# Attention, soft mixture of experts and a Mish layer on one core: the products of probabilities and values of a head pair written in two groups of five

## The chip, the cores and the metric

The kernel runs on one core of a Trainium2 chip. The metric is the device time of one execution in microseconds (us), as the median over several runs.

## The reference

Three layers follow one another. The attention has 4 batches, 8 heads, 576 positions and a head size of 64; the other two work on the 2304 rows of 512 that come out of it.

```python
q_rot, k_rot = (rotate(q), rotate(k))                     # rotary positions
scores = scale * np.matmul(q_rot, k_rot.transpose(0, 1, 3, 2))
attn = np.exp(scores - np.max(scores, axis=-1, keepdims=True))
attn = attn / (np.sum(attn, axis=-1, keepdims=True) + 1e-09)
x = np.matmul(attn, v)                                    # then (2304, 512)
# soft mixture of experts: softmax over rows and over slots of x @ phi,
# 8 experts of relu(slot_input @ w1) @ w2, mixed back
h = x @ w_in
out = (h * np.tanh(softplus(h))) @ w_out
```

## The kernel before

The attention works on 16 pairs of heads, one after the other; the loop index is `p`. For each pair there are nine score tiles. Tiles 0 to 7 are four blocks of 128 query positions for each of the two heads, and tile 8 holds the 64 remaining positions of both. Each tile goes through a fixed chain. TensorE (PE) multiplies queries and keys into PSUM (`s_mm`, lines 333 and 335; `s_mm2`, line 353, for tile 8). VectorE (DVE) takes the row maximum (line 361). ScalarE (ACT) takes the exponential with the sum (line 367). PE transposes the probabilities in blocks (lines 374, 388, 394, 396), and DVE or ACT copies the transposed blocks from PSUM into a tile `PT` (lines 398 to 401, 410, 413). There are two `PT` tiles for a pair: group 0 for the first 256 query positions, group 1 for the other 320.

The step that is in question here is `av(p, g, c)`: the product of the transposed probabilities with the values, for pair `p`, query group `g` and key block `c` of five. It issues two matmuls, one for each head (`h`). They write the lower and the upper 64 partitions of the same PSUM tile `m_av`, so each uses 64 of the array's 128 columns. The trace shows each such f32 matmul as two records (640 records for 320 matmuls). After the fifth block the tile is copied to `xts` (`evac`, line 410 or 413), the loads of the values for pair `p + 3` are issued (`load_v`), and `xback` (called X) transposes the result and multiplies it with `phi` (lines 449 to 457). The pool of `m_av` has one buffer, and so has `xts`. The score tiles have two PSUM buffers; the transposes, the rotated queries and keys, and X share three.

What is issued when is written in `PLAN`, one string for each of the nine steps of a pair. In it S, M and E are scores, maximum and exponential of the step's tile; T, K and R are transposes of the probabilities; V0 to V4 are `av` for group 0, W0 to W4 for group 1; X0 and X1 are `xback`; r, k and q bring the rotated inputs of the next pair through PE; a and d are their ACT and DVE halves; C is a step of a conversion of the weights `w_in` and `w_out` that runs beside the first eleven pairs or so; F is a step of the mixture's work for a batch that is done; L starts loads. A minus sign means that the action belongs to the pair before.

The written order is not the order in which an engine gets its instructions. The kernel is built with a planner (`schedule_with_timeline_sim=True`) that walks through a simulated time, and gives each engine the instruction that stands earliest in the program among those that it holds to be ready. `tc.keep_in_program_order(i)` adds one constraint: `i` comes behind the instruction that was traced just before it on its engine. It does not say that nothing may come between the two. In the attention the kernel uses it for little on PE; the last stage is pinned nearly throughout.

After the attention come the experts (lines 834 and 900), whose weights stream in by DMA, and the last layer (lines 1004 and 1038).

Of the kernel before, what the change touches and what calls it, by code (L numbers as in the profile page):

```python
# [24 lines left out]


PLAN = (
    "L T7- S M K1- E V3- V4-",
    "X0- R- C S M E",
    "S M E W0-",  # L30
    "F T0 r C S M E",
    "S a W1- W2- k F F W3- M T2 T1 E C",
    "S d q C M E",
    "S M C a E T3 W4-",
    "S a C T4 M E",
    "V0 K0 T5 d C F S F M T6 V1 E X1- d V2",
)

EVAC = {"T3": "d", "T4": "d", "K1": "a", "T0": "a", "T5": "a", "T2": "a"}
# [3 lines left out]
def kernel(  # L43
# [13 lines left out]
    nc = tc.nc  # L57
    NB, H, S, D = q.shape
    E, DM, F1 = w1.shape
# [148 lines left out]
    def load_v(p):  # L208
        b, h = divmod(2 * p, H)
        t = vs[p % 3]  # L210
        dma(
            out=t.rearrange("p h c d -> p h (c d)"),
            in_=v[b, h:h + 2, 0:512, :].rearrange("h (p c) d -> p h (c d)", c=4),
        )
        vt[p] = t
# [189 lines left out]
    def evac(dst, src, n, key=None):  # L405

        on = EVAC.get(key) or ("a" if load["a"] <= load["d"] else "d")
        if on == "a":
            load["a"] += n / 1.2 + 50
            nc.scalar.copy(dst, src)  # L410
        else:
            load["d"] += n / 0.96 + 65
            nc.vector.tensor_copy(dst, src)
# [3 lines left out]
    def av(p, g, c):  # L417
        b, hp = divmod(p, H // 2)
        n = 256 + g * R
        if c == 0:  # L420
            av_ps[p, g] = ps_a.tile([128, n], F32, tag="av", name="m_av")
        ps, pt = av_ps[p, g], PT[p, g]
        for h in range(2):
            o = 64 * h
            if c < 4:
                lhsT, rhs = vt[p][:, h, c, :], pt[:, 5 * h + c, :]
            else:
                lhsT, rhs = vrem[b % 2][:, hp, h, :], pt[:, 4, :]
            nc.tensor.matmul(ps[o:o + 64, :], lhsT=lhsT, rhs=rhs, start=(c == 0), stop=(c == 4))  # L429
        if c == 4:  # L430
            PT.pop((p, g))
            ps = av_ps.pop((p, g))
            xs = a4.tile([128, n], F32, tag="xts", name="xts")
            evac(xs, ps, n, f"X{g}")
            xts[p, g] = xs
            if g and p + 3 < NP:
                load_v(p + 3)
# [267 lines left out]
    def loads(p):  # L705
# [12 lines left out]
        "S": scores, "M": maxima, "E": expo,  # L718
        "T": lambda p, k: t_head(p, *tiles[k]), "K": t_keys, "R": lambda p, k: t_rem(p),
        "V": lambda p, k: av(p, 0, k), "W": lambda p, k: av(p, 1, k), "X": back,  # L720
        "r": lambda p, k: f_rem(p + 1), "k": lambda p, k: f_main(p + 1, "k"), "q": lambda p, k: f_main(p + 1, "q"),
        "a": lambda p, k: one(act_q), "d": lambda p, k: one(dve_q),
# [53 lines left out]
    ps = ps_m.tile([128, KDM, NSLOT], F32, tag="m", name="m_sit")  # L776
# [50 lines left out]
    for eg in range(2):  # L827
        for hf in range(2):
            end = eg == 1 and hf == 1
            for fh, cc in [(fh, cc) for fh in range(2) for cc in range(2)]:  # L830
                c = 2 * hf + cc
                for g in range(4):
# [3 lines left out]
                        rhs=parts[1, e, hf][0][:, cc * F1 + fh * 512:cc * F1 + fh * 512 + 512],  # L836
                        start=(eg == 0 and c == 0), stop=(eg == 1 and c == KDM - 1),
# [56 lines left out]
    for eg in range(2):  # L894
        for hf in range(2):
            for cc in range(4):
                c = 4 * hf + cc
                for g in range(4):
# [3 lines left out]
                        rhs=parts[2, e, hf][0][:, cc * DM:(cc + 1) * DM],  # L902
                        start=(eg == 0 and c == 0), stop=(eg == 1 and c == F1 // 128 - 1),
# [8 lines left out]
    ps = ps_m.tile([128, KDM, NSLOT], F32, tag="m", name="m_sot")  # L912
# [241 lines left out]
```

## Time and profile before

| | us |
|---|---|
| median of 3 runs | 672.29 |
| lowest and highest | 671.97, 673.31 |
| the profiled execution | 671.88 |
| its span in the trace | 670.1 |
| attention, until about | 389 |
| experts, until about | 436 |
| last layer, until the end | 670 |

In a row of the timeline stand the start, the time, the engine, the line, the operation with what it writes and reads, and how many such records are merged. "x2" at line 429 is the matmul of one head, "x4" both heads of a key block, "x12" three key blocks. The time in such a row reaches to the modelled end of the last record; how long PE was taken up is read from the start of one row to the start of the next. In square brackets stand the engine's idle time before the row and what ended it. A row of stretches gives, after the bounds and the length, the busy time (and count) of PE, PEld (weight load), DVE, ACT and POOL, then the granted clock of TensorE as a share, the DMA engines' mean busy share and GB/s.

### The profile page before, as it was taken

The numbers are of one execution on the slowest core, as the hardware profiler recorded it, in microseconds if no ns is written. First come the engines' busy times: TensorE is split into PE (matmuls) and PEld (weight loads), VectorE is DVE, ScalarE is ACT, GpSimd is POOL, SyncE is SP. The second block draws the span as 40 slices with busy tenths as digits, with TensorE's granted clock in tenths as the row PEclk, the third lists the DMA queues.
The fourth block names the chain that finished last, engine by engine and source line by source line (L and its number), as shares of the span: only waits on it lengthen the run. The fifth ranks groups of instructions, "written<-read, shape, count | busy, mean of one in ns | idle before, by whom it ended". The sixth has DMA issues, their size and how long they took to land.

```text
span 670.1 us, 11089 instructions
## 1 busy us (share of the span) xinstructions
PE 625.2 (93%) x4022; PEld 461.3 (69%) x4022; DVE 406.5 (61%) x824; ACT 336.4 (50%) x757; POOL 218.2 (33%) x263
## 2 busy tenths in 40 slices
PE   1598999989899999999999998999999999999997
PEld 1475677666577767777667653377787888888885
DVE  5777888786686866565756533177876533353342
ACT  2566776684776556665656411167765312222121
POOL 5758869755858644345400010000000000000000
PEclk9999999999999999999999999999999999999999
DMA  9678689868786965346359499962400200030004
GB/s 259 160 187 236 187 268 273 231 212 237 161 266 218 264 184 166 103 128 189 81 176 302 158 338 324 389 262 95 156 33 31 64 1 0 1 95 0 1 1 94
DMA packets 59607, 109.43 MB, mean 163 GB/s; under 512 B 12832, under 2 KB 25248, under 8 KB 59040
## 3 DMA queue, kind: packets, MB, share of 16 engines
q1 hardware_dynamic: 59552, 108.72, 54.2%
q8 instruction: 32, 0.52, 0.3%
q14 instruction: 23, 0.19, 0.1%
HBM read 70.25 MB, written 9.96 MB: 120 GB/s over the span
## 4 chain that ended last, share of the span: by engine, by line
PE 77%; DMA 9%; DVE 7%; ACT 2%; POOL 2%; issue 2%; SPq 1%; DVEq 0%; ACTq 0%; POOLq 0%
PE o_ps L1038 29%; PE m_av L429 13%; PE t L374 7%; PE s L333 5%; PE s L335 4%; PE hp L1004 3%; PE s L353 2%; DMA w<-in_moe_w_in_dram 2%; PE so_ps L900 2%; DMA w<-in_moe_w_dram 2%; DVE nmax L361 1%; PE m_lg L455 1%; PE tk L388 1%; PE m_k L285 1%; DMA w<-in_moe_w_out_dram 1%
## 5 line engine op out<-in xcount | busy, mean ns | idle before, releaser
L361 DVE TENSOR_REDUCE nmax<-s 128x1 f32<-128x576 f32 x144 | 108.0, 753 | 64.3 <-PE s L335 39.5
L367 ACT ACTIVATE P<-s,nmax 128x576 f32<-128x576 f32 x144 | 107.2, 745 | 36.3 <-DVE nmax L361 25.5
L1038 PE MATMUL o_ps<-wo_l,gh 128*128 128x512 f32 x288 | 112.9, 392 | 0.0
L1038 PE MATMUL o_ps<-wo_h,gh 128*128 128x512 f32 x288 | 112.9, 392 | 0.0
L1038 PE MATMUL o_ps<-wo_h,gl 128*128 128x512 f32 x288 | 100.7, 390 | 0.9 <-DVE gl L1019 0.9
L1011 ACT ACTIVATE room<-hp 128x512 f32<-128x512 f32 x72 | 43.0, 599 | 106.7 <-PE hp L1004 102.2
L333 PE MATMUL s<-qk_st 128*128 128x288 f32 x256 | 85.6, 349 | 10.3 <-ACT P L367 5.2
L374 PE MATMUL t<-cs,P 128*128 128x128 f32 x512 | 79.0, 282 | 4.8 <-ACT P L367 2.7
L410 ACT COPY PT<-t 128x512 f32<-128x512 f32 x92 | 53.5, 586 | 49.8 <-PE t L374 49.2
L429 PE MATMUL m_av<-PT,w 128*64 128x320 f32 (+1 forms) x384 | 73.3, 421 | 1.9 <-ACT PT L399 1.3
L374 PEld LDWEIGHTS t<-cs,P 128*128 128x128 f32 x512 | 59.6, 143 | 21.8 <-issue 9.7
L335 PE MATMUL s<-k_st,qk_st 128*128 128x288 f32 x256 | 73.8, 302 | 0.0
L333 PEld LDWEIGHTS s<-qk_st 128*128 128x128 f32 x256 | 49.9, 195 | 29.5 <-ACT P L367 9.1
L1013 DVE CAST gh<-room 128x512 fp32r<-128x512 f32 x49 | 20.9, 427 | 79.4 <-ACT room L1011 79.3
L1038 PEld LDWEIGHTS o_ps<-wo_h,gl 128*128 128x128 f32 x288 | 53.9, 188 | 13.2 <-DVE gl L1019 1.7
L231 POOL TENSOR_TENSOR w<-w,cs 128x512 f32<-128x512 f32 x34 | 45.2, 1332 | 54.1 <-PE m_k L285 46.6
L1038 PEld LDWEIGHTS o_ps<-wo_h,gh 128*128 128x128 f32 x288 | 54.1, 188 | 9.4
L1038 PEld LDWEIGHTS o_ps<-wo_l,gh 128*128 128x128 f32 x288 | 54.3, 189 | 9.0 <-DVE wo_l L891 0.2
L1019 DVE TENSOR_TENSOR gl<-room,gh 128x512 fp32r<-128x512 f32 x72 | 49.6, 691 | 4.6
L335 PEld LDWEIGHTS s<-k_st,qk_st 128*128 128x128 f32 x256 | 50.2, 196 | 0.0
L228 POOL TENSOR_TENSOR w<-w,cs 128x512 f32<-128x512 f32 x34 | 45.7, 1345 | 8.6 <-DMA w<-in_q_dram 2.9
L429 PEld LDWEIGHTS m_av<-PT,w 128*64 128x64 f32 x384 | 26.5, 136 | 23.0 <-issue 9.2
(175 smaller groups left out, 1011.5 us busy)
## 6 DMA issues: line engine op xcount, KB each, us to landing
w<-in_moe_w_dram SPq DMA_DIRECT2D x28, 1024.0 KB, 7.1
w<-in_moe_w_in_dram SPq DMA_DIRECT2D x16, 512.0 KB, 7.3
qk_st<-parth SPq DMA_DIRECT2D x46, 144.0 KB, 3.2
qk_st<-partl SPq DMA_DIRECT2D x46, 144.0 KB, 3.2
room<-in_moe_w_out_dram SPq DMA_DIRECT2D x12, 512.0 KB, 3.6
w<-in_q_dram SPq DMA_DIRECT2D x16, 256.0 KB, 5.2
w<-in_k_dram SPq DMA_DIRECT2D x16, 256.0 KB, 4.6
w<-in_moe_w_dram SPq DMA_DIRECT2D x16, 256.0 KB, 5.6
```

Source lines behind the costliest of these rows:

```text
L228: eng.tensor_tensor(out=tb, in0=src, in1=sin.to_broadcast([128, n, w]), op=ALU.mult)
L231: eng.tensor_tensor(out=dst, in0=sv, in1=cv, op=ALU.mult)
L333: nc.tensor.matmul(s[:, half, 0:288], lhsT=st[:, qc:qc + 128], rhs=st[:, KC + o:KC + o + 288], start=first, stop=False)
L335: nc.tensor.matmul(s[:, half, 0:288], lhsT=st[:, qc:qc + 128], rhs=k2_st[p % 2][:, o:o + 288], start=False, stop=last)
L361: nc.vector.tensor_reduce(out=stat[p][0][:, i:i + 1], in_=s[:, :, 0:288], axis=AX.XY, op=ALU.max, negate=True)
L367: nc.scalar.activation(out=P[p, t][:, h * S:(h + 1) * S].rearrange("p (a b) -> p a b", a=2), in_=s[:, :, 0:288], func=AF.Exp, bias=stat[p] ...
L374: nc.tensor.transpose(ps[:, j, :], P[p, t][:, blk * 128:(blk + 1) * 128], ident)
L410: nc.scalar.copy(dst, src)
L429: nc.tensor.matmul(ps[o:o + 64, :], lhsT=lhsT, rhs=rhs, start=(c == 0), stop=(c == 4))
L1011: pin(nc.scalar.activation(out=gg, in_=hp, func=AF.Mish))
L1019: pin(nc.vector.tensor_tensor(out=gl, in0=gg, in1=gh.bitcast(F32), op=ALU.subtract))
L1038: pin(nc.tensor.matmul(ops[i, n], lhsT=g_[:, cols], rhs=w_[f], start=(j == 0 and (x, k) == (0, 0)), stop=(j == NG - 1 and all(y[0] != n fo ...
```

## The change

The ten `av` steps of a pair stood in eight places of `PLAN`: V0, V1, V2 in the last step of their own pair, V3 and V4 in the first step of the next, W0 in its third step, W1 and W2, and W3, in the fifth, W4 in the seventh. They now stand in two: V0 to V4 at the end of the first step of the next pair, W0 to W4 in the fifth, ahead of k. And each matmul of `av` except the first of a group is kept behind the one before it.

```diff
 PLAN = (
-    "L T7- S M K1- E V3- V4-",
+    "L T7- S M K1- E V0- V1- V2- V3- V4-",
     "X0- R- C S M E",
-    "S M E W0-",
+    "S M E",
     "F T0 r C S M E",
-    "S a W1- W2- k F F W3- M T2 T1 E C",
+    "S a W0- W1- W2- W3- W4- k F F M T2 T1 E C",
     "S d q C M E",
-    "S M C a E T3 W4-",
+    "S M C a E T3",
     "S a C T4 M E",
-    "V0 K0 T5 d C F S F M T6 V1 E X1- d V2",
+    "K0 T5 d C F S F M T6 E X1- d",
 )
...
-            nc.tensor.matmul(ps[o:o + 64, :], lhsT=lhsT, rhs=rhs, start=(c == 0), stop=(c == 4))
+            mm = nc.tensor.matmul(ps[o:o + 64, :], lhsT=lhsT, rhs=rhs, start=(c == 0), stop=(c == 4))
+            if c or h:
+
+                tc.keep_in_program_order(mm)
```

## Rows read from the trace of the kernel before

**Rows 1.** The page's first part: busy time of each engine.
```profile
PE 625.2 (93%) x4022; PEld 461.3 (69%) x4022; DVE 406.5 (61%) x824; ACT 336.4 (50%) x757; POOL 218.2 (33%) x263
```
**Rows 2.** Stretches of the attention: early, middle, late.
```profile
84.00:106.00 22.00, 22.00 (x159) 15.95 (x159) 18.51 (x36) 16.31 (x39) 16.79 (x20) 1.00 0.91 259
...
172.00:194.00 22.00, 20.05 (x145) 14.61 (x144) 15.46 (x33) 14.69 (x36) 15.17 (x19) 1.00 0.87 240
...
282.00:304.00 22.00, 22.00 (x147) 15.29 (x146) 12.74 (x28) 13.43 (x33) 9.81 (x15) 1.00 0.47 121
```
**Rows 3.** Waits of PE, 128 to 200 us: total, times, longest.
```profile
PE t L374 <- DVE partl L273: 1.9, 1, 1.9
...
PE m_av L429 <- ACT PT L399: 1.3, 1, 1.3
```
**Rows 4.** PE's timeline: one pair's group 1 (320 columns), and what follows each piece.
```profile
277.12 0.75 PE L429 MATMUL m_av<-PT,w 128*64 128x320 f32 x2
277.81 0.40 PE L333 MATMUL s<-qk_st 128*128 128x288 f32 x1
...
279.47 1.84 PE L429 MATMUL m_av<-PT,w 128*64 128x320 f32 x12
281.24 0.66 PE L285 MATMUL m_k<-cs,w 128*128 128x128 f32 x4
281.82 0.75 PE L429 MATMUL m_av<-PT,w 128*64 128x320 f32 x2
282.51 0.66 PE L374 MATMUL t<-cs,P 128*128 128x128 f32 x4
```
**Rows 5.** PE's timeline: a tile 8, the next pair's group 0 (256 columns).
```profile
268.63 0.40 PE L353 MATMUL s<-qk_st 128*128 128x288 f32 x1
...
286.31 0.65 PE L429 MATMUL m_av<-PT,w 128*64 128x256 f32 x2
286.88 0.66 PE L374 MATMUL t<-cs,P 128*128 128x128 f32 x4
...
288.94 1.52 PE L429 MATMUL m_av<-PT,w 128*64 128x256 f32 x12
290.39 0.40 PE L353 MATMUL s<-qk_st 128*128 128x288 f32 x1
...
292.83 0.65 PE L429 MATMUL m_av<-PT,w 128*64 128x256 f32 x4
293.42 0.40 PE L333 MATMUL s<-qk_st 128*128 128x288 f32 x1
```
**Rows 6.** The last group 1, in the chain, and a copy from the timeline.
```profile
384.57 3.33 PE m_av L429 x20
...
384.55 0.37 ACT L399 COPY PT<-t 128x256 f32<-128x256 f32 x1 [1.74 <-DVE PT L398]
```
**Rows 7.** PE's timeline: four transposes ahead of scores, and ahead of a piece.
```profile
256.54 0.60 PE L374 MATMUL t<-cs,P 128*128 128x128 f32 x4
256.90 0.38 PE L333 MATMUL s<-qk_st 128*128 128x288 f32 x1
...
276.59 0.60 PE L374 MATMUL t<-cs,P 128*128 128x128 f32 x4
```
**Rows 8.** Timeline: an exponential, and scores that take its PSUM buffer.
```profile
277.90 0.75 ACT L367 ACTIVATE P<-s,nmax 128x576 f32<-128x576 f32 x1
...
282.92 0.38 PE L333 MATMUL s<-qk_st 128*128 128x288 f32 x1
```
**Rows 9.** Stretches around PE's longest wait of 128 to 200 us.
```profile
144.00:148.00 4.00, 2.13 (x18) 1.79 (x17) 3.61 (x6) 3.52 (x10) 3.33 (x4) 0.97 0.26 89
148.00:152.00 4.00, 4.00 (x22) 3.98 (x22) 2.35 (x3) 2.22 (x5) 4.00 (x4) 0.60 0.93 228
```
**Rows 10.** Stretches at the end of the attention.
```profile
376.00:386.00 10.00, 9.26 (x70) 6.87 (x71) 5.11 (x16) 3.96 (x10) 1.00 (x4) 1.00 0.26 95
386.00:396.00 10.00, 8.69 (x71) 5.92 (x68) 4.51 (x20) 2.08 (x8) 0.26 (x1) 1.00 1.03 385
```

## The prediction

> **What bounds the kernel now.** I read the engine totals first, then stretches of the attention, then the waits of PE, then PE's own timeline.
>
> The totals put PE at 93% of the span [rows 1], but an average says nothing of one stage, so I went on to stretches of 22 us, about one head pair. Late in the attention PE is busy for 22.00 of 22 us, while DVE has 12.74, ACT 13.43 and POOL 9.81 [rows 2]. PE is the bound there, with room everywhere else. From 84 to 106 us PE is full too, but DVE has 18.51 and the DMA engines 0.91 of their time. From 172 to 194 us PE has 20.05 of 22, with 15 us on POOL and 0.87 on DMA. So there are full stretches (84 to 128 and 190 to 380 us, together 234 us) and stretches in which others set the pace. The waits say the same: the long ones of PE after 128 us stand before 182 us, such as 1.9 us for a DVE subtraction and 1.3 us for a copy of probabilities [rows 3]; after that there is nothing over 0.5 us until the last pair.
>
> Since PE is always given something, a busy PE need not be an effective one. That is seen in its timeline. The reader should look at the starts in [rows 4]: a piece with one head's product ("x2") holds PE from 277.12 to 277.81, 0.69 us. Three key blocks of both heads ("x12", six times the work) hold it for 1.77 us. In group 0 one head takes 0.57 us, both heads of one block 0.59, and three blocks 1.45 [rows 5]. So the second head of a block is free if it follows the first, and a lone head costs as much as a pair of heads. From 0.69 for one block and 1.77 for three, a further block costs 0.54 us and each piece has a fixed 0.15 us. For group 0, 0.58 and 1.45 give 0.435 and 0.14.
>
> **What the change can take away.** I went through all pieces of line 429. Group 0 of every pair comes in four pieces or more (one head, one head, three blocks, one block; [rows 5] show three of them), 3.18 us in sum. The 15 groups 1 before the last come in three to five pieces, 58 in all; [rows 4] show three of the five pieces of the worst, 4.5 us, and the best are 3.14. Their mean is 3.77 us.
>
> One whole group would take 0.15 + 5 x 0.54 = 2.85 us (group 1) and 0.14 + 5 x 0.435 = 2.32 us (group 0). There is one whole group in the trace: the last of the attention holds the chain for 3.33 us, but its second head had to wait for a copy that started at 384.55 and took 0.37 us [rows 6]. Less those 0.4 us it is 2.9, as the sum says. So a pair can lose 3.77 - 2.85 = 0.92 us in group 1 and 3.18 - 2.32 = 0.86 us in group 0.
>
> Beside that each piece delays its neighbours. Four transposes hold PE for 0.36 us before scores (256.54 to 256.90), and for 0.53 before a piece (276.59 to 277.12, the first row of [rows 4]) [rows 7]: 0.17 us more. Behind scores the loss looks smaller. I take 0.1 us for each piece that goes, with ends 0 and 0.17. Group 1 loses 2.9 pieces (58 / 15 - 1), group 0 three: 0.29 and 0.30 us. If both groups became whole a pair would save 0.92 + 0.86 + 0.59 = 2.4 us (1.8 to 2.8).
>
> **What it will take away.** The plan's strings are only priorities. The pin orders the ten matmuls among themselves; it does not keep other work out. Each group must therefore be looked at by what can come between.
>
> *Group 1.* Its breaks have two causes. W0 stood in the third step, where its two heads become ready at different times: the transposed remainder is copied by DVE for one head and by ACT for the other. And W4 stood two steps behind W3, so it filled gaps as one head or one block, and earlier work took over after each. In the fifth step all ten inputs have long been copied, all ten rank ahead of k, T2, T1 and the next scores, and nothing of higher rank is left but that step's own scores. I expect one piece, at worst a lone head and the rest. Saving: 0.92 + 0.29 = 1.2 us.
>
> *Group 0.* Here the rank falls: all of it now stands behind K0, T5, the scores of tile 8, T6, X1, T7 and the next pair's first scores. It will still be used to fill gaps before those, and whatever of them becomes ready will still come between. Also, its second matmul reads what T3 leaves, and with the pins nothing of the group passes it. I expect it to stay in pieces and to lose about one of its three breaks: (0.86 + 0.30) / 3 = 0.4 us. Ends: 0 and 1.16.
>
> Sum: 1.6 us of PE time for a pair. Nothing is added: no instruction, no DMA. The value load of pair p + 3 waits for W3 as before, and PE reaches that at about the same point. X1 finds its input earlier. The `PT` tile of group 1 comes free earlier, that of group 0 is still read before T0 of the next pair, three steps on.
>
> How much of it reaches the end? In the full stretches PE waits for nobody, and the exponentials are ahead: the one at 277.90 frees its buffer by 278.7, and the scores that take this buffer start at 282.92 [rows 8], a slack of 4 us. So PE work that goes there is time that goes: 234 us / 21.8 us for a pair (tile 8 at 268.63 and 290.39 [rows 5]) = 10.7 pairs x 1.6 = 17.1 us. In the other stretches (40 to 84, 128 to 190 us) POOL, DMA or the conversion are late next; I count nothing there (ends: 0 and 1.6 for each of some five pairs, 8 us).
>
> The stages behind the attention move with it. Their weights need room that the attention gives back: DMA is 0.26 busy in the ten microseconds before its end and 1.03 right after [rows 10]. The transfers start when the attention ends, and the idle time before takes up what the last three pairs come earlier.
>
> Against the profiled execution's 671.88 us: 671.9 - 17.1 = 654.8. The median of the runs lies 0.4 us above that execution, less than I can resolve; I say 655. The forecast's own range is 646 to 664: group 0 between nothing and two breaks, and some gain in the other stretches.
>
> **Rivals.**
>
> *Both groups whole, and everywhere PE-bound.* 2.4 us x 15 pairs = 36 us: 636 (up to 42 us: 630). For it: inputs are ready early. Against it: group 0 is a filler by rank, and the stretches where DMA is at 0.9. Chance 0.11.
>
> *The change doesn't do what it says.* The planner breaks group 1 in its new place as it broke group 0 in its old one, or PE waits for as long as it saved. 672 (669 to 675). For it: the pin doesn't forbid insertion. Chance 0.12.
>
> *The fillers are missed: slower.* Today W4 and the first block of V stand as lone heads between transposes and scores, from 281.82 to 288.57, four pieces, 2 x 0.69 + 2 x 0.57 = 2.5 us. They bridge the time in which the three PSUM buffers of transposes and inputs wait for DVE and ACT. With W whole ahead of that stretch, and V held at its second matmul until T3 is copied, PE may wait there, and run V afterwards, when DVE and ACT starve. If it waits the whole 2.5 us and saves 1.6, a pair is 0.9 us longer: 15 x 0.9 = 13, so 685 (676 to 692). It decides from the point where the waits pass 1.6 us a pair. For it: DVE at 18.51 of 22 in the early stretch. Against it: the slack of [rows 8], and ACT and DVE near 13 of 22 later. Chance 0.17.
>
> *The clock falls.* Between 144 and 148 us PE was busy for 2.13 of 4 us, and from 148 to 152 us its granted clock was 0.60 on average [rows 9], between the full 2.4 GHz and the half. Such a stretch costs about 4 x 0.4 = 1.6 us. One a pair would cost 15 x 1.6 = 24 us: 655 + 24 = 679. Against it: it needs waits that the late stretches don't have. Chance 0.04. The Trainium skill has this as a rule (TensorE: Matmul & The Clock Gate, "Why this matters for your kernels"): gaps in which PE idles between bursts of matmuls send the clock to half. It speaks against two lumps with waits between them; by that rule, the trace agrees where its one long gap stands.
>
> **How the numbers follow.** Forecast 0.56, whole 0.11, nothing 0.12, fillers missed 0.17, clock 0.04. A difference under 0.2% (1.3 us) can't be told from none here. Faster: 0.56 + 0.11 = 0.67. Same: 0.12. Slower: 0.17 + 0.04 = 0.21. The range: from 638, which leaves out half of the first rival (0.05), to 682, which leaves out most of the fillers' (0.11); 0.16 in all.
>
> **What would show it.** Right: line 429 in the late attention shows rows of "x18" or "x20" with 320 columns, near 2.85 us, and the busy sum of a pair's PE falls while PE stays full; the pitch from one tile 8 to the next goes from 21.8 to about 20.1 us late in the attention. Group 0 wrong: it too is "x20". Fillers missed: PE waits for ACT or DVE copies, or for exponentials, of a microsecond and more in every pair between 200 and 380 us. Nothing: the same counts of "x2". The forecast is wrong in its base if the pieces heal and the pitch of the pairs stays.

## The result, and the profile after

| | before | after |
|---|---|---|
| median of the runs, us | 672.8 | 682.42 (678.15 to 684.94) |
| ratio | 1 | 1.013 (95% interval 1.0099 to 1.0161) |
| profiled execution, us | 671.88 | 681.91 |
| mean granted clock in it | 0.997 | 0.980 |

Slower by 1.3%, where 655 us were forecast. Everything happens in the attention: the first matmul behind it, `m_lt`, starts at 389.58 us before and at 399.79 after, and the stages that follow are as long as they were.

The totals hide it. First part of the page of after (engine, busy us, share, instructions), beside [rows 1]:

```profile
PE 626.1 (92%) x4022; PEld 470.8 (69%) x4022; DVE 408.1 (60%) x824; ACT 336.9 (50%) x757; POOL 217.8 (32%) x263
```

PE is as busy as before, although the pieces of line 429 did get fewer. PE's timeline of after, one pair's group 1 (320 columns) and the next group 0 (256), beside [rows 4, 5]:

```profile
267.95 0.75 PE L429 MATMUL m_av<-PT,v 128*64 128x320 f32 x2
268.63 0.33 PE L262 MATMUL m_rem<-cs,w 128*128 128x128 f32 x1
268.89 2.37 PE L429 MATMUL m_av<-PT,v 128*64 128x320 f32 x14
271.19 0.66 PE L285 MATMUL m_k<-cs,w 128*128 128x128 f32 x4
...
272.30 0.76 PE L429 MATMUL m_av<-PT,w 128*64 128x320 f32 x4
272.99 1.09 PE L374 MATMUL t<-cs,P 128*128 128x128 f32 x8
...
275.96 0.65 PE L429 MATMUL m_av<-PT,w 128*64 128x256 f32 x2
276.54 0.66 PE L374 MATMUL t<-cs,P 128*128 128x128 f32 x4
...
278.84 1.94 PE L429 MATMUL m_av<-PT,w 128*64 128x256 f32 x14
280.71 0.66 PE L374 MATMUL t<-cs,P 128*128 128x128 f32 x4
...
281.63 0.65 PE L429 MATMUL m_av<-PT,w 128*64 128x256 f32 x4
282.21 0.66 PE L458 MATMUL m_lg<-phi_sb,xts 128*128 128x64 f32 x4
```

The reader should look at the counts: a lone head (x2), seven matmuls (x14), the last block (x4), in both groups and in nearly every pair. Start to next start gives 0.68 + 2.30 + 0.69 = 3.67 us for group 1 and 0.58 + 1.87 + 0.58 = 3.03 for group 0. Work of lower rank stands in both gaps.

New are the waits. PE's waits of after from 50 to 401 us (total us, times, longest), beside [rows 3]:

```profile
PE s L353 <- ACT P L367: 4.2, 3, 3.4
PE s L333 <- DMA qk_st<-parth: 3.9, 2, 3.1
PE t L374 <- DVE partl L273: 3.7, 3, 3.4
...
PE m_q L285 <- POOL w L236: 1.5, 1, 1.5
```

The longest stand at 186.77 (3.42), 327.21 (3.09) and 153.48 us (3.37). Behind each the clock is down for some 6 us. Stretches of 4 us in after (busy time and instructions of PE, PEld, DVE, ACT, POOL, then the granted clock, the DMA share, GB/s):

```profile
324.00:328.00 4.00, 0.91 (x5) 0.82 (x4) 0.56 (x3) 0.37 (x1) 1.00 (x4) 0.70 0.65 147
328.00:332.00 4.00, 4.00 (x21) 3.97 (x20) 2.21 (x5) 2.02 (x5) 0.00 (x0) 0.50 0.00 0
332.00:336.00 4.00, 4.00 (x28) 2.83 (x28) 3.24 (x9) 2.43 (x7) 0.32 (x1) 0.95 0.02 4
```

A "full" PE at 0.50 does half of it: behind the wait at 186.77 us the matmuls of tile 8 follow each other at 0.24 us, behind the same tile's shorter wait in the kernel before at 0.13. PE's busy time times what is missing to a clock of 1, summed over all such stretches from 20 to 400 us, is 1.7 us before and 10.5 us after. In the totals this hides what the fewer pieces saved.

To see where time is lost I cut the attention at k's projection, which stands at the same place of each pair: the first mark (the second pair's k), the tenth mark of fifteen, and `m_lt`. "Early" is first to tenth mark, "late" from there to `m_lt`. The three of after, then those of before:

```profile
24.27 1.06 PE L285 MATMUL m_k<-cs,w 128*128 128x128 f32 x4
...
249.69 0.60 PE L285 MATMUL m_k<-cs,w 128*128 128x128 f32 x4
...
399.79 0.40 PE L583 MATMUL m_lt<-cs,c_all 128*32 128x128 f32 x2
```

```profile
24.44 1.06 PE L285 MATMUL m_k<-cs,w 128*128 128x128 f32 x4
...
239.26 0.60 PE L285 MATMUL m_k<-cs,w 128*128 128x128 f32 x4
...
389.58 0.39 PE L580 MATMUL m_lt<-cs,c_all 128*32 128x128 f32 x2
```

So all 10.6 us are lost early (214.8 to 225.4), and late nothing is won (150.3 to 150.1).

### The profile page after: what moved, and what is told of

The parts are those of the page before. It is cut to its first block, busy times and chain, and to the rows that moved or that the text cites. A ratio compares the mean times of both kernels' runs of the same rounds, so it can differ in the third digit from the quotient of the medians.

```text
span 680.1 us, 11095 instructions
## 1 busy us (share of the span) xinstructions
PE 626.1 (92%) x4022; PEld 470.8 (69%) x4022; DVE 408.1 (60%) x824; ACT 336.9 (50%) x757; POOL 217.8 (32%) x263
## 4 chain that ended last, share of the span: by engine, by line
PE 76%; DVE 8%; DMA 8%; ACT 3%; issue 2%; POOL 1%; SPq 1%; DVEq 0%; ACTq 0%; POOLq 0%
PE o_ps L1041 28%; PE m_av L429 11%; PE t L374 7%; PE s L333 5%; PE s L335 4%; DMA w<-in_moe_w_in_dram 3%; PE hp L1007 3%; DMA qk_st<-parth 3%; PE s L353 2%; PE h_ps L837 2%; PE so_ps L903 2%; PE m_lg L458 2%; DMA qk_st<-partl 1%; DVE nmax L361 1%; DVE PT L413 1%
## 5 line engine op out<-in xcount | busy, mean ns | idle before, releaser
L374 PE MATMUL t<-cs,P 128*128 128x128 f32 x512 | 81.3, 289 | 6.6 <-DVE partl L273 3.7
L374 PEld LDWEIGHTS t<-cs,P 128*128 128x128 f32 x512 | 61.8, 147 | 22.4 <-issue 11.7
L429 PE MATMUL m_av<-PT,w 128*64 128x320 f32 (+1 forms) x384 | 68.6, 425 | 0.0
L429 PEld LDWEIGHTS m_av<-PT,w 128*64 128x64 f32 x384 | 28.4, 139 | 22.0 <-issue 7.7
```

Source lines behind the costliest of these rows:

```text
L374: nc.tensor.transpose(ps[:, j, :], P[p, t][:, blk * 128:(blk + 1) * 128], ident)
L429: mm = nc.tensor.matmul(ps[o:o + 64, :], lhsT=lhsT, rhs=rhs, start=(c == 0), stop=(c == 4))
```

## The experiments

The ratios are medians of runs against the kernel before on the same chip; "early" and "late" are read off one profiled execution each.

| run | ratio (95%) | early | late |
|---|---|---|---|
| kernel before | 1 | 214.8 | 150.3 |
| the change, first comparison | 1.013 (1.010 to 1.016) | 225.4 | 150.1 |
| e5, the change again | 1.0101 (1.0068 to 1.0133) | 225.6 | 148.3 |
| e17, the change again | 1.0112 (1.0095 to 1.0129) | 225.9 | 149.5 |
| e1, weight load behind | 1.0028 (1.0007 to 1.0049) | 228.5 | 144.3 |
| e2, group 1 only | 1.0134 (1.0084 to 1.0184) | 227.4 | 150.7 |
| e3, group 0 only | 0.9958 (0.9935 to 0.9981) | 216.6 | 148.3 |
| e4, both glued | 1.0043 (1.0011 to 1.0076) | 222.1 | 149.5 |
| e6, group 0 whole | 0.9969 (0.9941 to 0.9996) | 220.8 | 145.3 |
| e7, group 1 a step later | 1.0043 (1.0009 to 1.0077) | 222.2 | 149.4 |
| e8, one wait filled | 1.0121 (1.0076 to 1.0166) | 226.1 | 148.1 |
| e9, early pairs only | 1.0119 (1.0063 to 1.0175) | 228.5 | 150.5 |
| e10, late pairs only | 0.9911 (0.9880 to 0.9942) | 217.6 | 144.4 |
| e11, late, group 0 whole | 0.9921 (0.9891 to 0.9951) | 215.0 | 144.2 |
| e12, late, both, 0 whole | 0.9973 (0.9944 to 1.0001) | 217.6 | 146.9 |
| e13, other order, no change | 1.0065 (1.0032 to 1.0098) | 218.0 | 151.2 |
| e14, other order 2, no change | 1.0010 (0.9981 to 1.0039) | 210.7 | 153.2 |
| e15, change, other order | 0.9891 (0.9848 to 0.9934) | 217.9 | 145.2 |
| e16, order of e14, late change | 0.9922 (0.9895 to 0.9949) | 209.7 | 148.4 |

The changed kernel's own split repeats within 0.5 us early and 1.8 late. Profiles of different kernels whose queues have the same order early lie up to 3.1 us apart there: before and e10 (214.8 and 217.6, every queue in the same order until 234 us), after and e1 (225.4 and 228.5). So an early part must differ by more than that to say anything. The profiled execution can lie off its kernel's median (e1's 5.4 us above, e14's 4.2 and e16's 3.4 below), so the ratio decides.

**Which half of the change, and is it a few waits or all pairs?** Theory A: a few long waits with a slow clock behind each. Theory B: every pair loses, since pieces no longer fill gaps.

e1: the load that a stage behind the attention needs is issued behind the stacked writes again.

```diff
         if p == NP - 4:
             assert not steps
+            fetch(ahead.pop(1), behind=True)
         if p == NP - 3:
...
-            for i in (0, 0, 2):
+            for i in (0, 2):
                 fetch(ahead.pop(i))
```

> The changed kernel, with one weight load (1 MB, into the room that the values' remainder of the third batch leaves) issued behind the twelve writes of stacked queries and keys of that pair instead of ahead of them. Theory A (a few long waits of PE, each with a clock fall behind it): the wait of 3.1 us before the scores at 327 us and the half clock until 332 us go, 3.1 + about 2.4 us, so 677 against 682 of the changed kernel; mean granted clock 0.985 instead of 0.98. Theory B (the loss is spread over all pairs because the pieces no longer fill gaps): the wait moves elsewhere, 681 to 683.

e2 and e3: the new priorities of one group only, no pin.

```diff
...
-    "S a W1- W2- k F F W3- M T2 T1 E C",
+    "S a W0- W1- W2- W3- W4- k F F M T2 T1 E C",
...
```

> Only group 1 (W0 to W4) moved to the fifth step; group 0 in its places of before; no pins. Theory A: it keeps the early weight load near 313 us, so a wait of 3 us and a clock fall there (5.5 us), keeps group 0's pieces ahead of tile 8's scores, so the wait of 3.4 us near 186 us shrinks to the 1.5 us of before, and saves about 0.1 to 0.2 us of pieces a pair: 674 to 677. Theory B: waits shared by the two groups alike, so half of the loss, 677 to 678, with no single wait over 2 us.

```diff
...
-    "L T7- S M K1- E V3- V4-",
+    "L T7- S M K1- E V0- V1- V2- V3- V4-",
...
```

> Only group 0 (V0 to V4) moved to the first step of the next pair; group 1 in its places of before; no pins. Theory A: no early weight load and no wait near 320 us; the wait before tile 8's scores of the seventh pair (3.4 us in the changed kernel) with its clock fall stays, 4 to 5 us, less 0.15 us of pieces a pair: 674 to 676. Theory B: half of the loss, 677 to 678, spread over the pairs.

e4: each group is to come in one piece, as the title of the change says; its nine later matmuls get the highest priority, and all ten are pinned.

```diff
+            if c or h:
+                with tc.high_priority():
+                    mm = nc.tensor.matmul(...)
...
+            tc.keep_in_program_order(mm)
```

> The changed kernel, with the first matmul of a group pinned too and the other nine at a higher priority of the planner: group 0 then runs in one piece in all pairs, group 1 in one or two. Theory A: PE work falls by a further 0.7 us (group 0) and 0.7 us (group 1) a pair, 15 to 20 us in all, of which the long waits take some back: 660 to 670. Theory B: with all pieces whole the gaps between score tiles are filled by nothing, PE waits grow in every pair: 682 to 695.

Group 1 alone costs as much as the whole change; group 0 alone gains 0.4%. Theory A had the load right (675.5 us for e1, forecast 677), but neither theory had the other three: e2 took 684.2 us (A 674 to 677, B 677 to 678), e3 671.2 (A 674 to 676, B 677 to 678), e4 677.4 (A 660 to 670, B 682 to 695). The pin does nothing: with the new priorities the compiled order of all five queues is the same with it and without. The load is worth 0.7 to 1.0% (1.0101 to 1.013 against 1.0028). SP's timeline of after shows how:

```profile
313.53 0.37 SPq L138 DMA_DIRECT2D w<-in_moe_w_dram  x1
313.99 0.47 SPq L317 DMA_DIRECT2D qk_st<-parth  x1
...
317.09 1.61 SPq L317 DMA_DIRECT2D k_st<-parth  x1
```

and of before:

```profile
304.29 0.47 SPq L317 DMA_DIRECT2D qk_st<-parth  x1
...
311.26 0.59 SPq L317 DMA_DIRECT2D qk_st<-partl  x1
311.95 0.55 SPq L138 DMA_DIRECT2D w<-in_moe_w_dram  x1
```

The 1 MB load takes the room of a value tile whose last reader is group 1's last block. Moved ahead of k, that block ends ahead of the twelve stacked writes, so the load overtakes them. The chain of waits of after holds what it costs:

```profile
313.99 7.14 DMA qk_st<-parth
...
321.21 5.41 DMA qk_st<-parth
...
327.21 0.58 PE s L333
```

The DMA view (tile, engine, count, KB, us from issue to landing) has the stacked writes at 5.2 to 7.5 us in after and at 2.5 to 3.3 before; one of them, after and then before:

```profile
k_st<-parth SPq DMA_DIRECT2D x1, 160.0 KB, 7.5
```

```profile
k_st<-parth SPq DMA_DIRECT2D x1, 160.0 KB, 3.1
```

In e1, with the load behind them, this wait is gone and the late pairs take 144.3 us. e4 leaves 1.0043. Group 0 is whole there (2.31 us where PE neither waits nor runs at a lower clock), group 1 is x16, x4 in ten of fifteen pairs and whole in five, and PE's waits over 0.3 us from 20 to 400 us sum to 35.8 us, against 18.4 before and 26.8 after.

**Group 0 whole, group 1 elsewhere, one wait filled.** e5 is the change again. e6 leaves group 1 in its old places, moves group 0, and gives its nine later matmuls the highest priority.

> The changed kernel once more, beside the others of this batch, as their measure: 1.010 to 1.016 of the kernel before, as in the first comparison (both theories). Its long waits of PE should stand at the same places: 3.4 us ahead of tile 8 of the seventh pair, 3.1 us for the stacked q and k near 327 us. If the place of a long wait changes from profile to profile, theory A (a few long waits, each with the clock at half behind it, make the loss) can't name its waits one by one.

```diff
...
+            if g == 0 and (c or h):
+                with tc.high_priority():
+                    mm = nc.tensor.matmul(...)
+                tc.keep_in_program_order(mm)
...
```

> Group 1 in the places of the kernel before; group 0 moved as in the change, and held together: its other nine matmuls get the highest priority behind the first, so it is one piece of ten in every pair, where the move alone leaves three. Ten in one piece should take PE 2.3 to 2.5 us instead of 3.03, 0.5 to 0.7 us less in each of 15 pairs. Theory A (the move of group 1 costs, through a few long waits): no new wait over 1.5 us comes up, since group 1 keeps its places, and the kernel gains those 8 to 10 us on top of the 0.4% of the move alone: 0.980 to 0.986 of the kernel before. Theory B (pieces fill gaps, and a lump leaves them open): the sum of PE's waits rises from 19 us by about as much as the pieces save, as it did when both groups were glued, and the time is 0.994 to 1.003.

```diff
...
-    "S d q C M E",
+    "S d q C M E W0- W1- W2- W3- W4-",
...
```

> Group 1 alone moved, grouped one step later than in the change (in the sixth step, behind the k projection of the next pair); group 0 as before. The 1 MB weight load that waits for the last matmul of group 1 then stands behind the twelve stacked writes of q and k again, as in the kernel before. Theory A: no wait for stacked q or k near 327 us, and the time is 0.998 to 1.006, well under the 1.013 of group 1 moved to the fifth step. Theory B (grouping itself costs, wherever it stands): 1.010 to 1.016 as in the fifth step.

```diff
+        if (p, t, blks[0]) == (6, 2, 0):
+            for _ in range(32):
+                with tc.high_priority():
+                    mm = nc.tensor.transpose(ps[:, 3, :], P[p, t][:, blk * 128:(blk + 1) * 128], ident)
+                tc.keep_in_program_order(mm)
```

> The changed kernel with 32 more transposes into a PSUM tile that has its result already (the same values again), in the seventh pair alone, just ahead of its tile 8: some 2.9 us of work for PE in the place where it waited 3.4 us for an exponential. Tile 8 is released by ACT's chain, not by PE, so it should start 12.0 us behind m_rem, as in both kernels. Theory A (the clock falls because PE stands still): the granted clock stays at 0.95 or more in the 8 us behind this wait, where it was 0.70, 0.50 and 0.94 in three stretches of 4 us, and the next pair's pitch is 2 to 3 us shorter. Rival: the clock falls for another reason (load, DMA, time): 0.5 again in the same place, although PE is busy. The time of the whole kernel moves by 2 us at most, 1.008 to 1.014.

e5 has its long waits where they were (3.37 us at 156, 3.39 at 189, 2.34 at 327 us). e6 came out as B has it, with new waits of 3.20, 2.66 and 2.24 us at 41, 66 and 108 us; e7 as A has it, without the wait near 327 us. Read by the marks they say the same: late e6 gains 5 us, early it loses 6 and e7 loses 7. So neither theory has the right cut: the loss is early, the gain late.

e8 tells what the clock is worth. The same stretches of e5, then of e8:

```profile
188.00:192.00 4.00, 2.82 (x14) 2.54 (x14) 1.80 (x4) 2.21 (x6) 3.97 (x4) 0.74 1.08 246
192.00:196.00 4.00, 4.00 (x26) 2.24 (x25) 0.93 (x5) 1.91 (x4) 1.33 (x2) 0.83 0.98 337
```

```profile
188.00:192.00 4.00, 4.00 (x35) 3.35 (x35) 1.68 (x3) 3.26 (x9) 3.63 (x4) 1.00 0.99 225
192.00:196.00 4.00, 2.75 (x23) 2.08 (x19) 2.39 (x6) 1.32 (x3) 1.51 (x2) 1.00 1.00 310
```

With PE kept busy in the wait the granted clock stays at 1.00 (2.4 GHz), so here its fall comes from PE standing still. The Trainium skill (TensorE: Matmul & The Clock Gate, "Why this matters for your kernels") says so of gaps between bursts, and this pair agrees. But the time that I expected back in the next pair did not come: tile 8 to tile 8 takes 25.03 us, against 24.88 in e5. PE now waits elsewhere:

```profile
194.20 0.37 PE L333 MATMUL s<-qk_st 128*128 128x288 f32 x1 [1.25 <-DMA qk_st<-partl]
```

The pair after that is shorter (18.36 us against 20.14), but by the tenth mark nothing is left of it: e8's early part is 226.1 us, the changed kernel's 225.4 to 225.9. The filler had a price of its own: tile 8 starts 12.7 us behind `m_rem`, where 12.0 were expected. So the 10.5 us of lost clock must not be added to the waits: here others set the pace. That a fall costs nothing is not shown by this one pair. ACT's timeline of after shows who, in the wait that e8 fills:

```profile
184.77 0.68 ACT L503 ACTIVATE w<-w 128x512 f32<-128x512 f32 x1 [2.83 <-DMA w<-in_moe_w_out_dram]
...
185.91 0.72 ACT L367 ACTIVATE P<-s,nmax 128x576 f32<-128x576 f32 x1
```

The conversion of a block of `w_out`, a weight of the last layer, waits for its load, and the exponential that tile 8 needs is queued behind it.

**Early against late.** Theory C: late, PE is the bound and fewer pieces are time; early, the change harms the queues that set the pace. Rival: the late gain is only catching up. All four kernels choose the priorities by the pair's number; in all of them the weight load stands behind the stacked writes.

```diff
         for i, step in enumerate(PLAN):
+            if p < 9 or p == 9 and not i:    # e9;  e10 to e12: p > 9 or p == 9 and i
+                step = NEW[i]
```

> The whole change in the first nine pairs alone, the places of the kernel before from the tenth pair on (the 1 MB weight load stands behind the stacked writes again). Theory C: in the early pairs POOL, DVE, ACT and the DMA queue set the pace, and the change reorders their queues, so the 8 to 11 us that k's first matmul of the eleventh pair came late (270 to 271 us instead of 260) stay, and nothing is won later: 681 to 685, 1.011 to 1.016 of the kernel before. Rival: the late pairs ran faster only because the early ones ran late (work that had been put off was done), so they catch up by themselves: 1.002 to 1.007.

> The whole change from the tenth pair on alone, with the 1 MB weight load issued behind the stacked writes as in the kernel before; the first nine pairs in the places of before, so that POOL's and SP's queues keep their order throughout. Theory C: in the late pairs PE is the bound and fewer pieces are time: the marks of k's first matmul went 85.6 us in four late pairs with the same change and the load behind, where the kernel before took 88.8, and the last pairs took 2 us less: minus 4 to minus 6 us, 0.991 to 0.994. Rival (the late gain was only catching up): 0.998 to 1.002.

> From the tenth pair on, group 0 alone in its new place and whole (ten in one piece); group 1 and the first nine pairs as before. Theory C: four late pairs took 83.4 us instead of 88.8 with group 0 whole in all pairs, and the end came 2.3 us closer behind them, so minus 6 to minus 8 us: 0.988 to 0.991. Rival (catching up): 0.997 to 1.001.

> As the run of the whole change in the late pairs, with group 0 whole besides, the load behind the stacked writes. Theory C, PE alone sets the late pairs: both savings add, 0.7 to 0.8 us a pair on top of the run without the whole group 0: minus 7 to minus 10 us, 0.985 to 0.990, the best of all. Rival: with both moved nothing is left to fill PE while it waits for DVE and ACT, and the second saving comes back as waits: 0.990 to 0.994, no better than group 0 whole alone.

C, clearly: the change in the early pairs alone costs 1.2%, in the late pairs alone it gains 0.9%. With the 0.7 to 1.0% of the load that makes 1.0 to 1.3%, which is what the whole change costs. e11 is as good as e10, a little short of C's 0.988 to 0.991: group 0 takes 2.31 us there, and group 1, left in its old places, comes out as x4, x12, x4, 3.15 us. e12 lies beyond both forecasts, on the rival's side (0.990 to 0.994): group 0 takes 2.31 us as well, but group 1 is x2, x14, x4 again, 3.67, and PE's late waits are 6.1 us against 2.3 in e10. They don't explain it: e11 has 7.3 us of them and is as fast as e10. What e12 loses is not settled. Marks of e10, beside those of after:

```profile
24.52 1.06 PE L298 MATMUL m_k<-cs,w 128*128 128x128 f32 x4
...
242.15 0.60 PE L298 MATMUL m_k<-cs,w 128*128 128x128 f32 x4
...
386.57 0.39 PE L593 MATMUL m_lt<-cs,c_all 128*32 128x128 f32 x2
```

**Why early?** The order of the queues gave the lead. In e3 ACT, POOL and SP are ordered as before and DVE differs in four places; the early part, 216.6 us, is within the spread. With group 1 moved (e2), another instruction than before stands at 379 of DVE's 824 places in the trace, at 384 of ACT's 757, 132 of POOL's 263 and 157 of SP's 386: the plan is made anew, and every engine gets another order. POOL in the second pair, after:

```profile
55.93 1.29 POOL L515 TENSOR_TENSOR w<-w,w 128x512 f32<-128x512 f32 x1 [1.15 <-ACT w L504]
57.18 1.28 POOL L228 TENSOR_TENSOR w<-w,cs 128x512 f32<-128x512 f32 x1
58.42 1.27 POOL L231 TENSOR_TENSOR w<-w,cs 128x512 f32<-128x512 f32 x1
59.65 1.29 POOL L516 TENSOR_TENSOR w<-w 128x512 f32<-128x512 f32 x1
...
61.56 0.72 POOL L236 TENSOR_TENSOR w<-w 128x256 f32<-128x256 f32 x1
```

and before:

```profile
54.55 1.28 POOL L228 TENSOR_TENSOR w<-w,cs 128x512 f32<-128x512 f32 x1
56.92 1.30 POOL L231 TENSOR_TENSOR w<-w,cs 128x512 f32<-128x512 f32 x1 [1.09 <-PE m_k L285]
...
58.86 0.90 POOL L236 TENSOR_TENSOR w<-w 128x256 f32<-128x256 f32 x1
```

Two steps of a weight's conversion (L515, L516) now stand around q's rotation, which ends at 62.28 instead of 59.76 us. q's projection waits 1.49 us for it:

```profile
62.34 0.78 PE L285 MATMUL m_q<-cs,w 128*128 128x128 f32 x4 [1.49 <-POOL w L236]
```

The stacked writes come later, and from this mark, the second, to the third it is 27.2 us instead of 21.8: half of the whole loss. From the sixth to the eighth mark, around the waits at 153 and 187 us, it is 56.6 us instead of 49.7; the other stretches give 1.7 us back. That these waits come from the order is read from the trace here; the runs that follow test the order as a whole.

But is it the order, or do groups as lumps make such waits in any order? Theory D: the order. Theory E: the lumps. e13 and e14 leave the groups in their old places and pin conversions behind what POOL was given ahead of them, in the second pair alone and in nine pairs; the plan is made anew by that. (They are conversions of `w_in` and `w_out`, the last layer's weights, though the first expectation calls them the experts'.) e15 is the change with e14's pin (the load stands behind the stacked writes there). e16 is e14 with the change in the late pairs.

```diff
...
+        if eng is nc.gpsimd and now[0] in (1,):      # e14 to e16: range(1, 10)
+            tc.keep_in_program_order(mul)
```

> The kernel before with both groups in their old places and its old pieces; one step of the expert weights' conversion on POOL is pinned behind the second pair's rotations, and the plan that follows orders the queues of all engines anew, as the change did (DVE, ACT, POOL and SP each differ from before in some 60 to 210 places). Theory D: the first nine pairs lose because the old order of the queues is lost, not because of the groups: from k's first matmul to that of the tenth pair on this list 220 to 228 us instead of 214.8, the rest as before (150.3): 1.005 to 1.015. Theory E: the groups as lumps open the waits: 213 to 217 us, 0.998 to 1.003.

> The same with the pin in each of nine pairs: a second, different order of the queues with the groups in their old places and old pieces. Theory D: again 220 to 228 us for the first nine pairs, 1.005 to 1.015; a spread between the two kernels of several us would say the same. Theory E: 213 to 217 us, 0.998 to 1.003.

> The change (both groups moved) with that pin in nine pairs: another order of the queues; the 1 MB weight load stands behind the stacked writes here. Theory E (lumps open the waits): the first nine pairs take 224 to 229 us as in all five kernels with group 1 moved everywhere, the rest 144 to 145: 1.002 to 1.006. Theory D (the order of the queues decides): anything from 214 to 230 us, off the other kernels with group 1 moved by 3 us or more in either direction.

> The order of the queues of the second neutral kernel (conversions pinned in nine pairs, groups as before up to the ninth pair) and the change from the tenth pair on, the load behind the stacked writes. If the two things are independent, as the split into early and late pairs says, the first nine pairs take 211 to 218 us (the two neutral kernels' values) and the rest 144 to 146 (the late change's): 355 to 364 us against 365.1 of before, 0.983 to 0.995 of it. If the order of the early queues also shifts what reaches the late pairs (the second neutral kernel took 153.2 there instead of 150.3), the late gain is smaller: 0.994 to 1.001.

> The changed kernel itself, a third time, beside the run of both: 1.009 to 1.016 as before. It tells whether the split of its time, 225.5 us for the first nine pairs and 148 to 150 for the rest, is the same in every profile: theory D needs a difference of 7.5 us between two orders of the queues to be larger than the spread of one kernel's profiles, which in two profiles was 0.2 us early and 1.8 late.

The order moves the time by itself: e13 loses 0.65% with both groups untouched. Where it loses is not shown: its early part is 218.0 us, where D wanted 220 or more and e10, in the order of before, has 217.6. e14 loses nothing, against D's forecast and as E had it. The case for D rests on e15: the same two groups, moved as in the change, gain 1.1% in e15's order and lose 0.3% in the change's own with the load behind (e1). That is 1.4% between two orders of the same work. E expected 1.002 to 1.006 for e15, so E is out as a rule. That lumps cost nothing early is not shown: e15's early part is 7 us longer than e14's, whose profiled execution was a short one. e16 met its first forecast in time, but not in its two parts: early it took 209.7 us instead of 211 to 218, late 148.4 instead of 144 to 146. e17 came out as expected. e15's pieces are nearly those of the change: group 0 is x2, x14, x4 until the last pair, group 1 is so in eight of fifteen pairs and x2, x18 or x16, x4 in the others. Its marks:

```profile
24.34 1.06 PE L285 MATMUL m_k<-cs,w 128*128 128x128 f32 x4
...
242.28 0.60 PE L285 MATMUL m_k<-cs,w 128*128 128x128 f32 x4
...
387.49 0.39 PE L586 MATMUL m_lt<-cs,c_all 128*32 128x128 f32 x2
```

The best four beat both kernels by about the same: e11 (667.3 us), e16 (667.8), e15 (668.0) and e10 (668.8).

## Why the prediction was wrong

**"I expect one piece, at worst a lone head and the rest": wrong.** Group 1 is three pieces, 3.67 us, where 2.85 were expected. Against the mean of 3.77 that is 0.10 us a pair, not 0.92. Four groups of the kernel before, three of them early, were x4, x12, x4 (3.14 us, heads together); there the new x2, x14, x4 is even longer. Why the planner puts k between the eighth and the ninth matmul stays open; the highest priority (e4) closes that gap in part of the pairs.

**Group 0 "to lose about one of its three breaks": right in the count,** four pieces to three. In size it saved 0.15 us (3.18 to 3.03) instead of a third of 0.86, because a lone head still stands ahead of the rest.

**The prices: right where PE is the bound.** In e10 the six groups 1 between the tenth mark and the last group take 21.2 us instead of 24.1, the seven groups 0 20.6 instead of 22.3, in seventeen pieces fewer. That is 4.6 us, and 0.1 us for each piece gone makes 6.3; measured 5.9 (150.3 to 144.4). So the fixed cost of a piece holds. The 0.1 us for its neighbours fits, but late parts of one kernel lie up to 1.8 us apart, too far to tell it from its ends (4.6 us with 0, 7.5 with 0.17). A whole group 0 measured 2.31 us (e11), forecast 2.32.

**"Nothing is added: no instruction, no DMA": true and beside the point.** The step went through the value load, X1 and the `PT` tiles, not through the load of the next stage's weights, which waits for the same last reader of `vrem`. That order was worth 0.7 to 1.0%.

**"In the other stretches ... I count nothing there (ends: 0 and 1.6 ...)": the step that decided.** The lower end was no loss. It took the order of POOL, DVE, ACT and SP as given. The priorities feed one plan for all engines; where others set the pace a new plan is a new draw, and here it cost 10.6 us early. The full stretches ahead of 240 us, which I had counted as PE-bound because PE was busy throughout, gave next to nothing: from the third to the sixth mark it was 65.6 us instead of 65.5, from the eighth to the tenth 45.4 instead of 46.0. In sum, from one profile each: late 6.0 us were won (150.3 to 144.3 in e1) where some seven pairs at 1.6 would have been 11, the load took 5.8 of them back (150.1), and early 10.6 were lost. That is 10.4 us, and `m_lt` came 10.2 late.

**The rivals.** "The fillers are missed" gave the right time (685) with the wrong place: it wanted waits of a microsecond in every pair between 200 and 380 us, and there was one such wait. "The clock falls" was sized at once a pair; it fell at four places, a consequence of the waits, and in e8, where one such fall was kept away, no time was left of it by the tenth mark. "The change doesn't do what it says" was half true: the groups are not whole. What the forecast called its sign, x18 or x20 rows late in the attention, did not appear there before the last group; one x18 row stands early, at 100.10 us.

## What to carry to other kernels

Where priorities feed a planner, compare the compiled order of every queue before trusting a sum over one engine: an edit that reorders only the engine it touches can be costed from the trace, one that reorders all of them is a new kernel in every stretch where PE does not set the pace. Look for loads whose room is freed by the moved work, however late their data is needed, and at what they now overtake. And make such a change only in the stretch that is bound by it: here that, with the load put behind, turned +1.0 to +1.3% into -0.9%. A full engine alone does not show such a stretch: from 84 to 106 us [rows 2] PE was as full as late, but DVE had 18.51 of 22 us and DMA 0.91, and little was won there; where it paid, DVE had 12.74 and DMA 0.47.

## What the runs showed of the hardware

Behind the waits of 3.1 to 3.4 us the granted clock was at 0.50 for about 6 us, and 32 repeated transposes in such a wait kept it at 1.00. It fell behind a wait of 1.87 us in the kernel before too (0.60 from 148 to 152 us [rows 9]), and not behind one of 1.50 us at 180.72. I had expected a clock that costs time wherever it falls, and in e8, without one of the falls, the early part was no shorter (226.1 us against 225.4 to 225.9). A 1 MB load issued 0.5 us ahead of twelve writes of 144 to 160 KB took their landing from about 3 us to between 5.2 and 7.5.
